# Second expert layer: where the halves of the next expert's weights are made, and three banks for the first products

## The chip, the core and the metric

The kernel runs on one core of a Trainium2 chip. The time is the device time of one execution in microseconds. Before the change it is 1087.37 us, the median of three runs (1087.16 to 1089.33). The core has five engines with a queue of instructions each, worked off in order: TensorE (PE in the rows; PEld is its weight load), VectorE (DVE), ScalarE (ACT), GpSimd (POOL) and SyncE (SP), which here issues the loads. Engines wait for each other by semaphores. TensorE writes its sums into PSUM, eight banks of 512 fp32 columns; ScalarE and VectorE read them there.

## The reference

Attention with normed queries and keys, then a first layer of eight experts with a free choice of expert for each token, then a second layer of eight experts in which each expert gets exactly 224 tokens. The change is in the second layer alone:

```python
def _moe2_ref(x, w_gate, w1, w2):          # x [1792, 768], w1 [8, 768, 1024], w2 [8, 1024, 768]
    cap = N // E                           # 224
    logits = x @ w_gate
    # pairs (token, expert) by falling logit; a token takes the first expert with room
    ...
    for e in range(E):
        mask = assigned == e
        h = np.maximum(x[mask] @ w1[e], 0.0)
        out[mask] = h @ w2[e]
```

All of it is fp32, and the result has to be near fp32 too.

## The kernel before

The second layer is `moe2`. It works the experts off one by one, in the order in which the assignment closes them (n = 0 to 7 below; "expert 6" is the seventh that is worked off). The assignment itself runs on all engines beside the experts, a few experts ahead (`pace`; lines up to L1908). An expert has 32 steps t.

*First products*, t = 0 to 15: h = relu(x W1), transposed. Eight products f, each of 128 rows of h by 224 tokens, summed over six pieces k of W1; two steps for a product. *Second products*, t = 16 to 31: h W2 in two halves of 112 tokens, each over eight pieces k of W2, in two column halves.

Experts 0 and 1 take fp32 operands as they are. From expert 2 on (`n >= NAT`) every operand is the sum of a high half, which TensorE takes at a higher rate, and the low rest. `split` (L2057 on) makes the two halves of one piece of a weight: ScalarE copies the piece into the high half (L2063, `w1h`, `w2h`), VectorE subtracts that from the piece into the low half (L2065, `w1l`, `w2l`). Then a first product is, per k, one wide matmul of the high half of W1 with both halves of x (448 columns, L2104) and a narrow one of the low half (224 columns, L2105); a second product is three matmuls (L2135 to L2137). What a first product leaves has to be summed and split as well (`relu2`): ScalarE copies one part (`hr`, L2110), VectorE adds the other (L2112), ScalarE makes the high half of relu (`hh`, L2114), VectorE the low half (`hl`, L2116). With the sum (L2112) the product's bank is free again.

The pieces of weights go through six buffers (`raws`, tiles `qkv`): 14 pieces an expert, six of W1 and then eight of W2, loaded in order by SP (`pump`, L2039), each as soon as the half six pieces earlier is made. W1's fourth piece is held back until the gather of the next expert's tokens has been issued on POOL, by a memset of one element there. There is one set of halves of W1 and one of W2, so those of the next expert can be written only when the present expert has read that piece for the last time.

`turn` (L2075) brings the gathered tokens of the next expert into x transposed, in four parts: three transposes into bank `px0`, then ScalarE's copy (`xx`, L2085) and VectorE's difference (L2088). All four use the one bank `px0`.

What sets the order around the change is the loop of `experts` (L2183 on). It runs at build time and issues each engine's instructions in the order that stands; it carries estimated clocks of the engines, with which `ahead(t)` decides whether a gather, a turn or a half is issued at a step. In the kernel before:

- `ahead` (L2187), from t = 17 on: a turn's transposes at one step, its copy and difference at the next; halves of W1 of the next expert at odd steps only, and not at a step on which transposes were issued, so in effect once the turns are done.
- After the 32 steps: the halves of W1 that are left, then the first two of W2 (L2259 to L2263).
- In the first products, at even t: `relu2` of the product before, and then half t/2 + 2 of W2 (L2210 to L2214).
- `product(f)` (L1989) gives product f the bank f mod 2 of `pg2`.

Of the kernel before, what the change touches and what calls it, by code (L numbers as in the profile page):

```python
# [22 lines left out]
N, DM, E, FF = 1792, 768, 8, 1024  # L23
# [1329 lines left out]
class Pace:  # L1353
# [49 lines left out]
    def work(self, eng, cost, ready=0.0):  # L1403

        clock = self.clock
        start = max(clock["p"], clock[eng], ready)
        self.until(start + SLACK if eng == "p" else min(start, clock["p"] + AHEAD))
        clock[eng] = max(start, clock[eng]) + cost
        return clock[eng] + SYNC
# [551 lines left out]
def moe2(tc, consts, qkv, x0, asn, w1, w2, y, out):  # L1961
# [10 lines left out]
    with ExitStack() as ctx:  # L1972
# [13 lines left out]
        zr = x0[0]  # L1986
        xgs = [p2.tile([CP, YW], F32, name=f"xg{i}") for i in range(2)]

        def product(f):  # L1989
            return pg2[f % 2][:, : 2 * CAP]  # L1990

        def first_product(f):

# [41 lines left out]
        def piece(i):  # L2035
            n, k = divmod(i, KD + KF)
            return n, k < KD, k if k < KD else k - KD
# [69 lines left out]
        def relu2(pg, f):  # L2107
            hr, hh = rows["hr"][f % NHR], rows["hh"]
            t = work("s", 0.36, max(done[f], there.get(("h", f - NHR), 0.0)))
            nc.scalar.activation(hr, pg[:, CAP:], AF.Copy)  # L2110
            t = work("v", 0.38, t)
            nc.vector.tensor_tensor(out=hr, in0=pg[:, :CAP], in1=hr, op=OP.add)  # L2112
            t = work("s", 0.33, t)
            nc.scalar.activation(hh[:, f, :], hr, AF.Relu)  # L2114
            there["h", f] = work("v", 0.36, t)
            nc.vector.scalar_tensor_tensor(hl[:, f, :], hr, 0.0, hh[:, f, :].bitcast(F32), op0=OP.max, op1=OP.subtract)  # L2116
# [37 lines left out]
        def experts(compact):  # L2154
# [26 lines left out]
                for _ in g:  # L2181
                    pass
            for n in range(E):  # L2183
                splits = iter(range(KD) if NAT <= n + 1 < E else ())
                turns, gathered, turned = [], 0, 0

                def ahead(t):  # L2187

                    nonlocal gathered, turned
                    if n + 1 == E:  # L2190
                        return
                    if known > n + 1 and gathered < 2:
                        gather(n + 1, gathered)
                        gathered += 1
                    elif t >= 17:
                        if turned < 4 and gathered > turned // 2 and ready[turned // 2] <= clock["p"]:
                            if len(turns) == turned:
                                turns.append(turn(n + 1, turned))
                                next(turns[turned])
                                return  # L2200
                            for _ in turns[turned]:
                                pass
                            turned += 1
                        if t % 2 and arrival and nload > nsplit + direct and arrival[piece(nsplit + direct)] <= clock["p"] + EARLY:
                            k = next(splits, None)
                            if k is not None:
                                split(n + 1, True, k)

                for t in range(32):
                    if n and t % 2 == 0 and 2 <= t <= 16:  # L2210
                        f = t // 2 - 1
                        relu(product(f)[:, :CAP], f) if n < NAT else relu2(product(f), f)
                    if n >= NAT and t % 2 == 0 and t // 2 + 2 < KF:
                        split(n, False, t // 2 + 2)  # L2214
                    if n and t == 3:
                        store(n - 1, 1)
                    if t == 25:
                        store(n, 0)
                    ahead(t)
                    pump()  # L2220
                    if t < 16:
                        if n:
                            f, a = divmod(t, 2)
                            for k in range(3 * a, 3 * a + 3):
                                acc(n, product(f)[:, :CAP], f, k) if n < NAT else acc2(n, product(f), f, k)
                        elif t < 6:

                            k, a = divmod(t, 2)
                            for f in range(4 * a, 4 * a + 4):
                                acc(n, first_product(f), f, k, True)  # L2230
                        elif t < 6 + KF:
                            f = t - 6
                            for k in range(3, KD):
                                acc(n, first_product(f), f, k, True)

                            for i in range(f - 1, f + 1) if f % 2 else ():
                                relu(first_product(i), i)
                    else:
                        gemm2(n, (t - 16) // 8, t % 8)
# [16 lines left out]
                        clock["p"] = max(clock["p"], ready[turned // 2])  # L2256
                    ahead(17)
                pump()
                for k in splits:  # L2259
                    split(n + 1, True, k)  # L2260
                if n + 1 >= NAT:
                    split(n + 1, False, 0)
                    split(n + 1, False, 1)  # L2263
            store(E - 1, 1)
            for r in room:
                r.close()
# [14 lines left out]
NAT = 2  # L2281
# [72 lines left out]
```

## Time and profile before

| | |
|---|---|
| median of 3 runs | 1087.37 us |
| the profiled execution | 1089.45 us |
| its span, first to last instruction | 1087.5 us |
| mean granted TensorE clock over the span | 0.958 |
| TensorE busy | 1016.0 us, 93% |
| VectorE busy | 601.5 us, 55% |
| ScalarE busy | 506.6 us, 47% |
| 16 DMA engines moved | 151.05 MB, mean 139 GB/s |

The span is read from the first to the last instruction of one execution; busy times are shares of it. The mean over the whole kernel says little of one stage: experts 2 to 7 of the second layer run from about 849 to 1075 us, and views with a window show that part alone. The granted clock is the share of TensorE's 2.4 GHz that the chip let through; 0.50 is its lower level of 1.2 GHz. In a row that shows idle time, the arrow names what ended it.

### The profile page before, as it was taken

What the parts mean: (1) busy time and instruction counts of PE and PEld (TensorE: products, weight loads), DVE (VectorE), ACT (ScalarE), POOL (GpSimd) and SP (SyncE); (2) the same over time, 40 slices, a digit from 0 to 9 for tenths busy, and PEclk for the clock granted to TensorE, in tenths of its full rate; (3) what the DMA queues carried; (4) which work ended last, traced back from release to release, by engine and by line L of the source; (5) the groups of instructions that cost most, each with busy time, mean ns of one, the idle gap of its engine ahead of it and who ended that gap; (6) DMA issues with size and microseconds to landing.
All of it is one profiled execution on the core that took longest, in us unless ns stands there. A gap on an engine that the chain in (4) does not pass through costs nothing. (4 is left out here: it accounts for less than half of the span.)

```text
span 1087.5 us, 19047 instructions
## 1 busy us (share of the span) xinstructions
PE 1016.0 (93%) x6224; PEld 785.1 (72%) x6224; DVE 601.5 (55%) x1664; ACT 506.6 (47%) x1127; POOL 238.3 (22%) x228
## 2 busy tenths in 40 slices
PE   7999999999999699999999998949999999999895
PEld 6555555555565588888888997738575789889885
DVE  5776877877875931111322121585778766565470
ACT  3777677777776322221352222641212555464460
POOL 5444333333323410001060111010111011021000
PEclk7899999999999899999999999867999999899998
DMA  6566556566556036436630011015930854775540
GB/s 154 123 145 146 130 140 146 129 145 147 124 154 200 5 92 246 157 137 238 222 117 32 31 59 36 16 52 219 323 101 18 266 181 150 237 228 157 182 143 28
DMA packets 80898, 151.05 MB, mean 139 GB/s; under 512 B 14254, under 2 KB 53422, under 8 KB 80752
## 3 DMA queue, kind: packets, MB, share of 16 engines
q1 hardware_dynamic: 75552, 126.06, 39.4%
q0 software_dynamic: 5200, 23.33, 6.7%
q8 instruction: 56, 0.92, 0.4%
q14 instruction: 90, 0.74, 0.2%
HBM read 110.69 MB, written 17.44 MB: 118 GB/s over the span
## 5 line engine op out<-in xcount | busy, mean ns | idle before, releaser
L205 DVE TENSOR_REDUCE nm<-sp 112x1 f32<-112x448 f32 x192 | 117.8, 618 | 56.9 <-PE sp L204 29.2
L211 ACT ACTIVATE e<-sp,nm 112x448 f32<-112x448 f32 x192 | 121.8, 634 | 54.1 <-DVE nm L205 34.9
L2104 PE MATMUL bank<-xx,w1h 128*128 128x448 f32 x288 | 101.9, 403 | 13.9 <-DVE hr L2112 13.8
L219 PE MATMUL tp<-ident,e 112*112 112x112 f32 x768 | 112.0, 269 | 0.6 <-DVE et L222 0.6
L219 PEld LDWEIGHTS tp<-ident,e 112*112 112x112 f32 x768 | 82.0, 135 | 26.4 <-issue 20.0
L232 PE MATMUL op<-et,qkv 112*64 112x448 f32 x384 | 99.3, 564 | 0.0
L225 ACT ACTIVATE et<-tp 112x448 f32<-112x448 f32 x144 | 78.4, 546 | 36.6 <-PE tp L219 35.1
L908 PE MATMUL po<-w2h,hh 128*128 128x384 f32 x240 | 85.9, 358 | 0.1
L200 PE MATMUL sp<-bt,at 128*112 128x448 f32 x188 | 85.6, 455 | 0.4 <-DMA bt<-cut 0.3
L880 PE MATMUL pg<-w1h,xh 128*128 128x512 f32 x180 | 75.8, 421 | 7.4 <-PEq L1192 6.0
L909 PE MATMUL po<-w2l,hh 128*128 128x384 f32 x240 | 81.8, 341 | 0.0
L911 PE MATMUL po<-w2h,hl 128*128 128x384 f32 x240 | 79.9, 338 | 0.0
L2105 PE MATMUL bank<-xx,w1l 128*128 128x224 f32 x288 | 79.1, 275 | 0.0
L2104 PEld LDWEIGHTS bank<-xx,w1h 128*128 128x128 f32 x288 | 57.2, 198 | 26.3 <-DVE hr L2112 21.2
L2143 POOL DMA_INDIRECT out_dram<-x,ids x16 | 17.2, 1074 | 254.3 <-ACT x L2142 129.3
L137 POOL TENSOR_TENSOR xn<-qkv,rr 112x512 f32<-112x512 f32 x47 | 48.0, 1053 | 112.7 <-DVE rr L128 112.7
L882 PE MATMUL pg<-w1h,xl 128*128 128x512 f32 x180 | 71.9, 399 | 0.0
L881 PE MATMUL pg<-w1l,xh 128*128 128x512 f32 x180 | 71.8, 399 | 0.0
L200 PEld LDWEIGHTS sp<-bt,at 128*112 128x112 f32 x188 | 33.9, 181 | 47.3 <-issue 32.0
L2135 PE MATMUL bank<-w2h,hh 128*112 128x384 f32 x192 | 66.3, 345 | 0.0
L896 DVE TENSOR_TENSOR hl<-ph,hh 128x512 fp32r<-128x512 f32 x30 | 20.7, 690 | 80.6 <-ACT hh L893 48.8
L2137 PE MATMUL bank<-w2h,hl 128*112 128x384 f32 x192 | 64.7, 337 | 0.0
(438 smaller groups left out, 2180.6 us busy)
## 6 DMA issues: line engine op xcount, KB each, us to landing
qkv<-in_moe_w_dram SPq DMA_DIRECT2D x88, 384.0 KB, 6.0
qkv<-in_moe_w_dram SPq DMA_DIRECT2D x36, 512.0 KB, 4.5
raw<-in_moe_w_dram SPq DMA_DIRECT2D x24, 512.0 KB, 6.6
bt<-cut SPq DMA_DIRECT2D x96, 112.0 KB, 2.3
at<-cut SPq DMA_DIRECT2D x96, 112.0 KB, 2.3
w1s<-in_moe_w_dram SPq DMA_DIRECT2D x12, 512.0 KB, 6.6
w2s<-in_moe_w_dram SPq DMA_DIRECT2D x16, 384.0 KB, 9.1
qkv<-in_v_dram SPq DMA_DIRECT2D x12, 448.0 KB, 6.7
```

Of the source, the lines that this page charges most:

```text
L200: nc.tensor.matmul(sp, lhsT=at[:, h, cs], rhs=bt[:, h, :], start=h == 0, stop=h == 1)
L205: nc.vector.tensor_reduce(out=st["nm"][:, n : n + 1], in_=sp, axis=AX.X, op=OP.max, negate=True)
L211: nc.scalar.activation(e, st.pop(("s", n)), AF.Exp, bias=st["nm"][:, n : n + 1], accum_out=st["sm"][:, n : n + 1])
L219: nc.tensor.transpose(tp[:, kc, :], e[:, kc * CP : (kc + 1) * CP], ident[:CP, :CP])
L225: nc.scalar.activation(dst, tp, AF.Copy)
L232: nc.tensor.matmul(st["op"][h * D : (h + 1) * D, :], lhsT=raws[i // 2][:, 2, 2 * (i % 2) + h, kc * D : (kc + 1) * D], rhs=st["et"][:, h, k ...
L880: nc.tensor.matmul(pg, lhsT=xh[:, k, :], rhs=w1h[:, k, fs], start=k == 0, stop=False)
L908: nc.tensor.matmul(po[n], lhsT=hh[:, k, :], rhs=w2h[:, kk, cs], start=kk == 0, stop=False)
L909: nc.tensor.matmul(po[n], lhsT=hh[:, k, :], rhs=w2l[:, kk, cs], start=False, stop=False)
L911: nc.tensor.matmul(po[n], lhsT=hl[:, k, :], rhs=w2h[:, kk, cs], start=False, stop=kk == KF - 1)
L2104: nc.tensor.matmul(pg, lhsT=h[:, k, fs], rhs=xx[:, k].rearrange("p a c -> p (a c)"), start=k == 0, stop=False)
L2105: nc.tensor.matmul(pg[:, :CAP], lhsT=l[:, k, fs], rhs=xh[:, k, :], start=False, stop=k == KD - 1)
```

## The change

Three things are changed, all for experts 2 to 7.

1. `ahead` issues halves at every step from 17 on, beside a turn too, in the order of the pieces: the six of W1, and from t = 26 on those of W2 as well, where the present expert's second products are past the piece (`what[2] <= t - 25`; for expert 2's own W2 not, since the memory is then still expert 1's). What is left of W1 and the first two of W2 follow after the 32 steps as before, and what is left of W2 goes beside the first products, one at each even step.
2. `relu2` pauses after the sum, and the half of W2 is issued there: between `hr` with its sum and `hh`, no longer behind `hl`.
3. The first products go round three banks, the two of `pg2` and `px0`, which the turns use in the second products.

```diff
-        def product(f):
-            return pg2[f % 2][:, : 2 * CAP]
+        def product(n, f):
+            if n < NAT:
+                return pg2[f % 2][:, :CAP]
+
+            return (pg2 + [px0])[f % 3][:, : 2 * CAP]
...
             nc.vector.tensor_tensor(out=hr, in0=pg[:, :CAP], in1=hr, op=OP.add)
+            yield
             t = work("s", 0.33, t)
             nc.scalar.activation(hh[:, f, :], hr, AF.Relu)
...
-                splits = iter(range(KD) if NAT <= n + 1 < E else ())
...
                                 turns.append(turn(n + 1, turned))
                                 next(turns[turned])
-                                return
-                            for _ in turns[turned]:
-                                pass
-                            turned += 1
-                        if t % 2 and arrival and nload > nsplit + direct and arrival[piece(nsplit + direct)] <= clock["p"] + EARLY:
-                            k = next(splits, None)
-                            if k is not None:
-                                split(n + 1, True, k)
+                            else:
+                                for _ in turns[turned]:
+                                    pass
+                                turned += 1
+                        what = piece(nsplit + direct)
+                        if what[0] == n + 1 and (what[1] or n >= NAT and t > 25 and what[2] <= t - 25) and nload > nsplit + direct and arrival[what] <= clock["p"] + EARLY:
+                            split(*what)
...
-                        relu(product(f)[:, :CAP], f) if n < NAT else relu2(product(f), f)
-                    if n >= NAT and t % 2 == 0 and t // 2 + 2 < KF:
-                        split(n, False, t // 2 + 2)
+                        sums = relu2(product(n, f), f) if n >= NAT else relu(product(n, f), f)
+                        if sums:
+                            next(sums)
+                    what = piece(nsplit + direct)
+                    if n >= NAT and t % 2 == 0 and what[:2] == (n, False):
+                        split(*what)
+                    if n >= NAT and t % 2 == 0 and 2 <= t <= 16:
+                        next(sums, None)
...
-                for k in splits:
-                    split(n + 1, True, k)
-                if n + 1 >= NAT:
-                    split(n + 1, False, 0)
-                    split(n + 1, False, 1)
+                while n + 1 >= NAT and (piece(nsplit + direct)[1] or piece(nsplit + direct)[2] < 2):
+                    split(*piece(nsplit + direct))
```

Line numbers rise by three from `first_product` on and by four behind `relu2`: the wide first product is L2104 before and L2107 after, the sum L2112 and L2115, the halves L2063 and L2065 before and L2066 and L2068 after.

How the order moves on VectorE beside expert 6's second products, before (`xx` a turn's difference, `w1l` and `w2l` low halves of expert 7's weights; `bank_11364` is `px0`):

```order
L2088 TENSOR_TENSOR xx<-bank_11364,xx 128x3x112 x4
L2065 TENSOR_TENSOR w1l<-qkv_88,w1h 128x1024 x2
L2065 TENSOR_TENSOR w1l<-qkv_87,w1h 128x1024 x3
L2065 TENSOR_TENSOR w1l<-qkv_88,w1h 128x1024
L2065 TENSOR_TENSOR w2l<-qkv_88,w2h 128x768 x2
```

And at the same place in the changed program, up to the first products of expert 7:

```order
L2068 TENSOR_TENSOR w1l<-qkv_88,w1h 128x1024
L2091 TENSOR_TENSOR xx<-bank_11364,xx 128x3x112
L2068 TENSOR_TENSOR w1l<-qkv_88,w1h 128x1024
L2068 TENSOR_TENSOR w1l<-qkv_87,w1h 128x1024
L2091 TENSOR_TENSOR xx<-bank_11364,xx 128x3x112
L2068 TENSOR_TENSOR w1l<-qkv_87,w1h 128x1024 x2
L2091 TENSOR_TENSOR xx<-bank_11364,xx 128x3x112
L2068 TENSOR_TENSOR w1l<-qkv_88,w1h 128x1024
L2091 TENSOR_TENSOR xx<-bank_11364,xx 128x3x112
L2068 TENSOR_TENSOR w2l<-qkv_88,w2h 128x768 x2
L2068 TENSOR_TENSOR w2l<-qkv_87,w2h 128x768 x3
L2068 TENSOR_TENSOR w2l<-qkv_88,w2h 128x768 x2
```

The four differences stood in a row ahead of all halves; now one or two halves of W1 stand ahead of each, and seven halves of W2 follow. TensorE's transposes stand where they stood, two steps apart.

ScalarE at the change from expert 6 to expert 7, before (`x` is the copy of a finished result for the store):

```order
L2063 ACTIVATE w2h<-qkv_88 128x768 x2
L2063 ACTIVATE w2h<-qkv_87 128x768
L2110 ACTIVATE hr_12573<-bank_11359 128x224
L2114 ACTIVATE hh<-hr_12573 128x224
L2063 ACTIVATE w2h<-qkv_87 128x768
L2142 ACTIVATE x_89<-bank_11363 112x384
L2142 ACTIVATE x_89<-bank_11361 112x384
L2110 ACTIVATE hr_12574<-bank_11360 128x224
L2114 ACTIVATE hh<-hr_12574 128x224
L2063 ACTIVATE w2h<-qkv_87 128x768
L2110 ACTIVATE hr_12575<-bank_11359 128x224
```

And changed:

```order
L2066 ACTIVATE w2h<-qkv_88 128x768 x2
L2066 ACTIVATE w2h<-qkv_87 128x768 x3
L2066 ACTIVATE w2h<-qkv_88 128x768 x2
L2113 ACTIVATE hr_12546<-bank_11359 128x224
L2066 ACTIVATE w2h<-qkv_88 128x768
L2118 ACTIVATE hh<-hr_12546 128x224
L2146 ACTIVATE x_89<-bank_11363 112x384
L2146 ACTIVATE x_89<-bank_11361 112x384
L2113 ACTIVATE hr_12547<-bank_11360 128x224
L2118 ACTIVATE hh<-hr_12547 128x224
L2113 ACTIVATE hr_12548<-bank_11364 128x224
L2118 ACTIVATE hh<-hr_12548 128x224
```

Before, three halves of W2 stand ahead of the first sum and one behind each of the five products that follow; changed, seven stand ahead and one follows, between `hr` and `hh`. The third product reads bank 11364, the turns' bank.

VectorE at the start of expert 3's first products in the changed program (`ns` is a small reduction of the assignment, which TensorE's matmul L1779 takes right behind product 0; before, it stood beside expert 1's second products):

```order
L2068 TENSOR_TENSOR w2l<-qkv_87,w2h 128x768
L2068 TENSOR_TENSOR w2l<-qkv_88,w2h 128x768 x3
L2068 TENSOR_TENSOR w2l<-qkv_87,w2h 128x768 x3
L1776 TENSOR_REDUCE ns<-u 128x8
L1782 SCALAR_TENSOR_TENSOR w<-w,u 128x64
L1784 TENSOR_REDUCE k<-w 128x8
L2115 TENSOR_TENSOR hr_12546<-bank_11359,hr_12546 128x224
L2068 TENSOR_TENSOR w2l<-qkv_88,w2h 128x768
```

Three small steps of the assignment have moved so, to behind the seventh half of W2: this one for expert 3, and two others for experts 4 and 5.

## Rows read from the trace of the kernel before

**Rows 1.** The page, costliest groups: busy, mean ns of one, idle before with releaser.

```profile
L2104 PE MATMUL bank<-xx,w1h 128*128 128x448 f32 x288 | 101.9, 403 | 13.9 <-DVE hr L2112 13.8
```

**Rows 2.** Stages by window: length, busy by engine, granted clock, DMA share, GB/s.

```profile
849.49:868.60 19.11, 17.02 (x98) 14.52 (x97) 14.10 (x24) 9.84 (x22) 1.04 (x2) 1.00 0.86 270
...
886.98:907.24 20.26, 17.74 (x97) 15.77 (x97) 13.80 (x24) 10.56 (x23) 1.04 (x2) 0.92 0.89 288
...
925.33:946.41 21.08, 18.59 (x98) 17.00 (x97) 13.26 (x23) 10.87 (x23) 1.04 (x2) 0.84 0.86 280
...
964.78:984.04 19.26, 16.74 (x97) 14.36 (x97) 12.42 (x22) 10.56 (x23) 1.04 (x2) 1.00 0.92 294
...
1002.00:1022.84 20.84, 17.74 (x97) 15.70 (x97) 12.72 (x23) 10.64 (x24) 1.04 (x2) 0.92 0.88 285
1022.84:1040.80 17.96, 17.96 (x111) 17.71 (x109) 9.57 (x12) 10.50 (x16) 0.97 (x1) 1.00 0.34 102
1040.80:1058.30 17.50, 16.31 (x97) 14.35 (x97) 12.48 (x23) 10.26 (x23) 0.94 (x1) 1.00 0.38 133
```

**Rows 3.** TensorE in order of time, first products: start, length, idle before.

```profile
892.86 0.47 PE L2104 MATMUL bank<-xx,w1h 128*128 128x448 f32 x1 [1.93 <-DVE hr L2112]
...
969.65 0.47 PE L2104 MATMUL bank<-xx,w1h 128*128 128x448 f32 x1 [0.92 <-DVE hr L2112]
...
1002.00 0.36 PE L2104 MATMUL bank<-xx,w1h 128*128 128x448 f32 x1
...
1005.68 0.27 PE L2105 MATMUL bank<-xx,w1l 128*128 128x224 f32 x1
1008.46 0.47 PE L2104 MATMUL bank<-xx,w1h 128*128 128x448 f32 x1 [2.51 <-DVE hr L2112]
```

**Rows 4.** ScalarE in order of time, first products of expert 6.

```profile
1006.27 0.84 ACT L2063 ACTIVATE w2h<-qkv 128x768 fp32r<-128x768 f32 x1 [1.91 <-DMA qkv<-in_moe_w_dram]
...
1012.05 0.34 ACT L2110 ACTIVATE hr<-bank 128x224 f32<-128x224 f32 x1
1013.47 0.39 ACT L2114 ACTIVATE hh<-hr 128x224 fp32r<-128x224 f32 x1 [1.08 <-DVE hr L2112]
```

**Rows 5.** VectorE in order of time, same stretch: one round of the loop.

```profile
1013.06 0.38 DVE L2112 TENSOR_TENSOR hr<-bank,hr 128x224 f32<-128x224 f32 x1
1013.90 0.39 DVE L2116 SCALAR_TENSOR_TENSOR hl<-hr,hh 128x224 fp32r<-128x224 f32 x1 [0.46 <-ACT hh L2114]
1014.63 0.96 DVE L2065 TENSOR_TENSOR w2l<-qkv,w2h 128x768 fp32r<-128x768 f32 x1 [0.34 <-ACT w2h L2063]
1015.51 0.38 DVE L2112 TENSOR_TENSOR hr<-bank,hr 128x224 f32<-128x224 f32 x1
```

**Rows 6.** A window of two microseconds in expert 4's first products, columns as rows 2.

```profile
934.00:936.00 2.00, 2.00 (x9) 1.87 (x8) 1.20 (x3) 1.48 (x3) 0.79 (x1) 0.50 0.74 168
```

**Rows 7.** TensorE in order of time, transposes beside expert 6's second products.

```profile
1023.89 0.45 PE L2081 MATMUL bank<-ident,xg 112*128 112x112 f32 x3
...
1026.27 0.45 PE L2081 MATMUL bank<-ident,xg 112*128 112x112 f32 x3
```

**Rows 8.** ScalarE in order of time, second products of expert 6.

```profile
1023.92 0.39 ACT L2114 ACTIVATE hh<-hr 128x224 fp32r<-128x224 f32 x1 [0.46 <-DVE hr L2112]
...
1032.96 5.79 ACT L2063 ACTIVATE w1h<-qkv 128x1024 fp32r<-128x1024 f32 x6
1039.08 0.85 ACT L2063 ACTIVATE w2h<-qkv 128x768 fp32r<-128x768 f32 x1 [0.33 <-DMA qkv<-in_moe_w_dram]
```

**Rows 9.** VectorE in order of time: expert 1's, then expert 6's second products.

```profile
827.84 0.50 DVE L2088 TENSOR_TENSOR xx<-bank,xx 128x336 fp32r<-128x336 f32 x1
828.26 1.20 DVE L1853 TENSOR_SCALAR g<-i,k 128x112 bf16<-128x112 bf16 x7
...
1034.04 6.90 DVE L2065 TENSOR_TENSOR w1l<-qkv,w1h 128x1024 fp32r<-128x1024 f32 x6 [1.53 <-ACT w1h L2063]
```

**Rows 10.** Loads into the six buffers, 1000 to 1048 us.

```profile
DMA to landing us min/median/max: 3.7/5.0/7.0
```

More of the change, by code (lines that the diff above doesn't have):

```diff
@@ L2224, in experts @@
                             for k in range(3 * a, 3 * a + 3):
-                                acc(n, product(f)[:, :CAP], f, k) if n < NAT else acc2(n, product(f), f, k)
+                                (acc if n < NAT else acc2)(n, product(n, f), f, k)
                         elif t < 6:
```

## The prediction

> **What bounds the kernel now.** I read the page's list of the costliest groups first: the idle time of TensorE in the stage that is changed is 13.9 us in front of the wide first products, 13.8 of it ended by VectorE's sum of the product halves (`hr`, L2112) [rows 1]. Then the time by stage, cut at the first matmul of each stage of experts 2 to 7 [rows 2]. The reader is to see two things there. In the second products TensorE is busy all the time (17.96 of 17.96 us), so nothing can be won there. In the first products it is not: the six stages last 19.11, 20.26, 21.08, 19.26, 20.84 and 17.50 us, 118.05 in all.
>
> What they would last without waits is read where TensorE runs freely, in the first two products of expert 6 [rows 3]: from the first wide matmul (1002.00) to the twelfth narrow one (1005.68) pass 3.68 us, and the next would be issued 0.10 later. So 12 pairs take 3.78 us, one pair 0.315, the 48 pairs of a stage 15.1; with 0.2 for the change of stage, 15.3. Six such stages are 91.8 us. The stages lose 118.05 - 91.8 = 26.25 us.
>
> Where it goes: product 2 of expert 6 waits 2.51 us for VectorE [rows 3]. Product f needs the bank of product f - 2, and that sum stands on ScalarE and VectorE behind halves of W2 whose weights have not landed (ScalarE waited 1.91 us for the DMA) [rows 4]. After that the two engines run a loop: from VectorE's sum at 1013.06 to the next at 1015.51 are 2.45 us [rows 5], because ScalarE's `hh` waits for the sum (1.08 us), the half of W2 stands behind `hh`, VectorE's half behind ScalarE's, and the next sum behind that [rows 4, 5]. TensorE needs only 6 x 0.315 = 1.89 us a product. The long waits have a second price. Two microseconds after such a wait the granted clock stood at 0.50, the 1.2 GHz level [rows 6]; the stages of experts 3, 4 and 6, where a wait was 1.93 to 2.51 us long, show 0.92, 0.84 and 0.92, the others 1.00 [rows 2, 3]. The largest waits of expert 5, 0.92 us, left it at 1.00 [rows 2, 3]. At (1 - clock) x length that is 1.6 + 3.4 + 1.7 = 6.7 us of the 26.25.
>
> **The change, part by part.** *Third bank.* Product f now needs the bank of f - 3, so its sum may end 1.9 us later than before. *Order in the products.* ScalarE's half of W2 stands between `hr` and `hh`, so it waits for no sum, and VectorE's row per product is sum, half, `hl`. That is 0.38 + 0.96 + 0.39 = 1.73 us, under 1.89, and ScalarE's 0.34 + 0.84 + 0.39 = 1.57 is too [rows 4, 5]: the loop is gone even for expert 2, which keeps five halves beside its products. *Earlier halves.* For experts 3 to 7 seven of the eight halves of W2 stand before the first sum and one behind it. All six stages should come down to 15.3 us: 26.25 us gained. I bound this: at most all of it; at least what the third bank alone would leave if the 2.45 us loop stayed, 8 x 2.45 = 19.6 a stage, which is nothing. I take all of it, since only one product per expert has a half beside it.
>
> *What hides the moved halves.* They now lie beside the second products, where VectorE was busy 9.57 of 17.96 us and ScalarE 10.50 [rows 2]. By the order of the changed program VectorE there makes 6 halves of W1, 4 turns, and then 6 to 7 halves of W2. W2's half k may be written only when TensorE has last read piece k, one step of about 1.05 us after another, and one half costs VectorE 0.96: it keeps up. The seventh piece of W2 is loaded into a buffer that the first half of W2 frees. With T the start of the second products, TensorE is done with piece 0 after 9.5 steps of 1.05 us, four turns of 2.38 - 2.10 = 0.28 and the 1.4 of waits worked out below [rows 7], at T + 12.5. ScalarE's half ends 0.85 later, VectorE's another 0.96, at 14.3. A load took 3.9 us (VectorE's first half of W1 ended at 1034.04 + 1.15 = 1035.19, ScalarE had the next piece at 1039.08) [rows 8, 9], so it lands at 18.2, and VectorE has made its half at 20.0, about 0.7 us into the next first products, which begin at 17.96 + 1.38 = 19.3. Their first sum is due 1.9 us in at the earliest. This costs nothing, but the cover is thin (rival C).
>
> *What the moved halves delay.* This is the price. The turns (three transposes into one bank, ScalarE's copy, VectorE's difference) used to come first on both engines, with the halves of W1 behind them; TensorE's transposes were 1026.27 - 1023.89 = 2.38 us apart and waited for nothing [rows 7]. Now two halves of W1 stand between two turns, and the next turn's transposes wait until VectorE has read the bank, with all second products queued behind them on TensorE. Six halves took VectorE 6.90 us, 1.15 each, and a difference 0.42 to the next start (827.84 to 828.26) [rows 9]. Two halves and a difference are 2.72 us against 2.38: each later turn waits 0.34. The first: `hh` of the last product starts at T + 1.08 (1023.92 - 1022.84) [rows 7, 8], the first half of W1 0.3 later at 1.4, VectorE's 1.08 behind it (1034.04 - 1032.96) [rows 8, 9] at 2.48, its difference at 3.63, done at 4.13 (0.50). The second transposes are due at 1.05 + 2.38 = 3.43 and wait 0.70. Together 0.70 + 0.34 + 0.34 = 1.38 us for each of experts 2 to 6, 6.9 us. Expert 1's second products (plain fp32, no halves) are longer, so its turns stand further apart and mostly find the bank free; of the 1.38 I put 0.4 there, an estimate between none and all of it. Bounds: nothing if VectorE runs ahead; if ScalarE's copy (0.39, as `hh`) never overlaps either, the two later waits are 2 x 1.15 + 0.50 + 0.39 - 2.38 = 0.81 each and the first 0.70 + 0.39 = 1.09, 2.71 an expert and 13.6 in all for five. I take 7.3, the value from back-to-back rows.
>
> *Waits that move.* Small matmuls of the assignment move from second into first products: no sum changes, but three of them now stand behind VectorE's seventh half (C). POOL's gathers keep their place ahead of the first products' stores, and the register loads on SP still come an expert early: nothing.
>
> Sum: 26.25 - 7.3 = 18.95 us. The profiled execution took 1089.45 us, so it would take 1070.5; the median of the runs is 2.08 us below it, so I predict 1087.37 - 18.95 = **1068.4 us**.
>
> A rule that speaks against the change: the Trainium skill, "TensorE: Matmul & The Clock Gate", section "HAM oscillation", reports that a second set of PSUM banks gave a kernel no further gain once its matmuls ran on. By it the third bank would be worth nothing here. The trace differs: it shows 13.8 us of waits for exactly that bank [rows 1].
>
> **The rivals.** *A, the forecast*: 1068.4, own range 1064 to 1073. *B, the turns don't wait*: VectorE ran in front of its order wherever rows let me see it; then 1087.37 - 26.25 = 1061.1. Against it: the 2.72 against 2.38 us come from back-to-back rows. *C, a late load*: loads took 3.7 to 7.0 us [rows 10]. At 7.0 the seventh piece lands at T + 21.3, 2.0 us into the first products; its two halves (0.85 + 0.96) and a small step of VectorE's, no longer than a sum (0.38), later an assignment matmul of experts 3, 4 and 5 that is due at 1.9 can run at 4.2. That is a wait of 2.3 us, long enough for the clock to fall, another 1.7 as in expert 6's stage [rows 2]. Three times 4.0 is 12: 1080.4. *D, no change*: C together with the turns' upper bound gives back 12 + 13.6 = 25.6 of 26.25: 1086.7. *E, slower by the clock*: if the waits of 0.3 to 0.7 us at the turns made the clock fall as expert 4's wait did, (1 - 0.84) x 21.08 = 3.4 us each time, twice beside each of five experts' second products, 34 us would be lost: 1102.4. It decides from six such stretches on. Against it stand expert 5's waits of up to 0.92 us at a clock of 1.00 [rows 2, 3].
>
> For E speaks the same page of the Trainium skill, section "A second HAM failure mode": frequent short idles between groups of matmuls, while banks are cycled, let the clock swing. By that the time would be E's; expert 5's stage contradicts it here.
>
> **How the numbers follow.** A 0.63, B 0.14, C 0.15, D 0.03, E 0.05. A run of this kernel is told from no change from about 0.2% (2.2 us) on. A, B and C are faster: 0.92; D is the same: 0.03; E slower: 0.05. The range reaches from B, 1061, to C, 1081.
>
> **What would show it.** Right: first-product stages of 15.2 to 15.6 us at clock 1.00, next to no wait of the wide first products for `hr`; second products of 19.0 to 19.7 us with waits of the transposes for `xx`, some 7 us in all, the first of a stage the longest; ScalarE's DMA waits beside the first products gone. Wrong: transposes that don't wait (B); assignment matmuls of experts 3 to 5 that wait 2 us for VectorE (C); a clock below 1.00 in second products (E); or the 2.45 us step between sums surviving beside most products, by which the gain itself would be missing.

## The result, and the profile after

The changed kernel took 1077.77 us, the median of eight runs (1072.99 to 1085.25), beside 1089.52 us for eight runs of the kernel before. The ratio is 0.9911, 95% interval 0.9894 to 0.9929: a gain of 9.7 us by the ratio, 11.75 by the medians, 11.03 between the two profiled executions (1089.45 and 1078.42). Forecast were 18.95. The direction was right, but four tenths of the gain (by the medians) to half of it (by the ratio) are missing: the time lies outside the forecast's own range of 1064 to 1073, between rivals A (1068.4) and C (1080.4) and nearer to C.

The wide first products, which were held up 13.8 us before [rows 1], now wait for nothing. From the page:

```profile
L2107 PE MATMUL bank<-xx,w1h 128*128 128x448 f32 x288 | 93.7, 381 | 0.0
```

The stages by window, columns as in [rows 2]. In order: expert 2's first and second products, the first products of experts 3 and 4, expert 5's first and second products, expert 6's first products.

```profile
850.39:865.89 15.50, 15.50 (x102) 14.68 (x99) 12.17 (x23) 9.46 (x23) 1.05 (x2) 1.00 0.79 270
865.89:885.24 19.35, 18.61 (x111) 17.48 (x109) 15.38 (x21) 14.08 (x20) 2.88 (x4) 1.00 0.67 199
885.24:901.75 16.51, 15.45 (x99) 14.46 (x98) 10.17 (x38) 7.58 (x18) 1.05 (x2) 1.00 0.65 242
...
921.21:941.97 20.76, 17.04 (x99) 15.89 (x99) 9.03 (x30) 7.47 (x18) 1.06 (x2) 0.92 0.55 190
...
961.31:977.76 16.45, 15.77 (x105) 14.86 (x104) 8.06 (x21) 7.58 (x18) 1.06 (x2) 1.00 0.63 236
977.76:997.10 19.34, 18.62 (x111) 17.46 (x109) 14.90 (x18) 14.08 (x20) 2.87 (x3) 1.00 0.67 199
997.10:1012.28 15.18, 15.18 (x97) 14.34 (x97) 7.13 (x16) 7.29 (x18) 1.06 (x2) 1.00 0.69 255
```

Two things are to be seen. Where TensorE runs freely (expert 6, 15.18 us; expert 7, 15.19) the first products take what the forecast said. Experts 3, 4 and 5 do not: 16.51, 20.76 and 16.45. And every second-product stage of experts 2 to 6 takes 19.34 to 19.46 us where it took 17.96 to 18.38, with TensorE idle for 0.45 to 0.75 us of each by its matmul rows.

| read from the stages | before | after | difference | forecast |
|---|---|---|---|---|
| first products, experts 2 to 7 | 118.05 | 99.59 | -18.46 | -26.25 |
| second products, experts 2 to 6 | 90.76 | 96.83 | +6.07 | +6.9 |
| second products, expert 1 | 25.53 | 26.22 | +0.69 | +0.4 |

The rest between the two spans, +0.6, lies ahead of and behind these stages. So the first products miss 7.8 us. The second products came out 0.8 us better than forecast: nine of the 16 small matmuls of the assignment that stood beside those of experts 2 to 6 are no longer there. TensorE's waits show where the 7.8 us went, in order of time (start, length, idle before):

```profile
866.94 0.45 PE L2084 MATMUL bank<-ident,xg 112*128 112x112 f32 x3
870.04 0.51 PE L2084 MATMUL bank<-ident,xg 112*128 112x112 f32 x3 [0.57 <-DVE xx L2091]
872.73 0.51 PE L2084 MATMUL bank<-ident,xg 112*128 112x112 f32 x3
...
888.35 0.17 PE L1779 MATMUL bank<-ns,ones 128*128 128x8 bf16 x1 [1.06 <-DVE ns L1776]
...
926.98 0.17 PE L1878 MATMUL bank<-fb,ut 128*128 128x8 bf16 x1 [3.72 <-DVE fb L1874]
...
964.31 0.22 PE L1858 MATMUL bank<-place,g 128*112 128x32 bf16 x1 [0.68 <-DVE g L1853]
```

The last three are the assignment matmuls of rival C, one in each of experts 3, 4 and 5. Expert 4's wait seen from ScalarE, VectorE and SyncE:

```profile
925.01 0.84 ACT L2066 ACTIVATE w2h<-qkv 128x768 fp32r<-128x768 f32 x1 [4.86 <-DMA qkv<-in_moe_w_dram]
```

```profile
925.88 0.96 DVE L2068 TENSOR_TENSOR w2l<-qkv,w2h 128x768 fp32r<-128x768 f32 x1 [4.74 <-ACT w2h L2066]
926.76 0.17 DVE L1874 TENSOR_SCALAR fb<-busyn 128x8 bf16<-128x8 f32 x1
```

```profile
916.43 0.33 SPq L2057 DMA_DIRECT2D qkv<-in_moe_w_dram  x1
```

The seventh piece of W2 was issued at 916.43, and ScalarE could take it at 925.01. VectorE waits for ScalarE's half; the small step `fb` of the assignment stands behind VectorE's; TensorE stands before `fb`. About a microsecond later the granted clock was down to 0.50, the 1.2 GHz level:

```profile
928.50:930.50 2.00, 2.00 (x9) 1.87 (x8) 0.04 (x1) 0.36 (x1) 0.97 (x1) 0.50 0.99 309
```

How long that piece takes is in the DMA view. First the landing times (the last number) when the window holds only this issue, for experts 4, 6 and 7 (experts 3 and 5: 5.7 each); then packets, megabytes and share of the 16 engines by queue in the two microseconds from the issue, expert 4's and expert 7's (q0 carries gathers and stores, q1 the loads):

```profile
qkv<-in_moe_w_dram SPq DMA_DIRECT2D x1, 384.0 KB, 8.5
...
qkv<-in_moe_w_dram SPq DMA_DIRECT2D x1, 384.0 KB, 6.1
...
qkv<-in_moe_w_dram SPq DMA_DIRECT2D x1, 384.0 KB, 3.3
...
q0 software_dynamic: 81, 0.33, 70.6%
q1 hardware_dynamic: 11, 0.03, 9.9%
...
q1 hardware_dynamic: 63, 0.19, 43.7%
q0 software_dynamic: 36, 0.11, 15.7%
```

Expert 7 is the last, so no tokens are gathered beside its load and no weights of a next expert follow it. It alone, with 3.3 us, is near the forecast's 3.9.

### The profile page after: what moved, and what is told of

The parts are those of the page before. It is cut to its first block, busy times and chain, and to the rows that moved or that the text cites. A ratio compares the mean times of both kernels' runs of the same rounds, so it can differ in the third digit from the quotient of the medians.

```text
span 1076.4 us, 19072 instructions
## 1 busy us (share of the span) xinstructions
PE 1009.3 (94%) x6224; PEld 780.4 (73%) x6224; DVE 600.0 (56%) x1664; ACT 511.4 (48%) x1127; POOL 233.9 (22%) x228
## 5 line engine op out<-in xcount | busy, mean ns | idle before, releaser
L2107 PE MATMUL bank<-xx,w1h 128*128 128x448 f32 x288 | 93.7, 381 | 0.0
L2140 PE MATMUL bank<-w2l,hh 128*112 128x384 f32 x192 | 64.7, 337 | 0.0
```

The lines of the kernel that those rows point to most:

```text
L2107: nc.tensor.matmul(pg, lhsT=h[:, k, fs], rhs=xx[:, k].rearrange("p a c -> p (a c)"), start=k == 0, stop=False)
```

## The experiments

Theory 1: what is missing is rival C (a late seventh piece, with an assignment step behind its half), and the turns' price is as forecast. The rivals to it are in the expectations. The sums of six first-product and five second-product stages (experts 2 to 6) are from each kernel's one profile, the ratios from its comparison with the kernel before. Where a load's landing decides, the stages differ from run to run (the profiles of experiments 5, 8, 9 and 12 are their slowest runs: 1080.12, 1084.27, 1067.83 and 1079.94), so verdicts go by the ratios.

| kernel | median us | ratio (95%) | first | second |
|---|---|---|---|---|
| before (medians of the five comparisons) | 1086.96 to 1089.52 | | 118.05 | 90.76 |
| changed | 1077.77 | 0.9911 (0.9894 to 0.9929) | 99.59 | 96.83 |
| 1 seventh half behind the sum | 1069.55 | 0.9828 (0.9810 to 0.9847) | 91.99 | 97.21 |
| 7 gather later | 1069.48 | 0.9842 (0.9827 to 0.9857) | 92.11 | 96.77 |
| 2 one half between turns | 1075.03 | 0.9888 (0.9869 to 0.9907) | 101.01 | 93.22 |
| 3 edits 1 and 2 | 1068.98 | 0.9819 (0.9799 to 0.9840) | 96.33 | 92.00 |
| 5 turns on two banks | 1077.36 | 0.9900 (0.9879 to 0.9922) | 108.99 | 90.28 |
| 6 edits 1 and 5 | 1062.30 | 0.9773 (0.9758 to 0.9788) | 92.01 | 90.36 |
| 4 third bank alone | 1077.37 | 0.9903 (0.9884 to 0.9922) | 101.07 | 94.21 |
| 13 order alone | 1076.75 | 0.9894 (0.9870 to 0.9918) | 104.46 | 91.35 |
| 9 bank and order | 1064.70 | 0.9791 (0.9778 to 0.9804) | 93.80 | 91.40 |
| 14 edits 9 and 5 | 1065.54 | 0.9803 (0.9788 to 0.9819) | 92.67 | 90.78 |
| 8 changed, two banks | 1077.58 | 0.9898 (0.9880 to 0.9915) | 104.73 | 96.82 |
| 10 edit 6, two banks | 1065.63 | 0.9799 (0.9786 to 0.9813) | 94.34 | 90.40 |
| 11 edit 6, old order | 1073.94 | 0.9883 (0.9866 to 0.9899) | 93.45 | 97.97 |
| 12 edit 6, both old | 1077.47 | 0.9897 (0.9882 to 0.9913) | 99.77 | 97.99 |

**1. The seventh half behind the first sum.**

```diff
-... t > 25 and what[2] <= t - 25)
+... t > 25 and what[2] <= min(t - 25, 5))
...
-if n >= NAT and t % 2 == 0 and what[:2] == (n, False):
+if n >= NAT and t % 2 == 0 and t and what[:2] == (n, False):
```

> The changed kernel, but the seventh half of W2 (and the eighth) is issued behind the first sum, beside the first products; the sixth stays ahead. Theory 1 (of the 18.95 us forecast some 7.8 are missing in the first products of experts 3, 4 and 5, where 1.06, 3.72 and about 1 us are waited by an assignment matmul for a small step of VectorE that stands behind the seventh half, whose piece lands 5.8 to 8.6 us after its issue; in expert 4 the clock falls after it): all six first-product stages 15.2 to 15.6 us at clock 1.00 (the changed kernel: 15.5, 16.5, 20.8, 16.5, 15.2, 15.2); second products unchanged at 19.3; time some 7 to 8 us under the changed kernel's 1077.8, near 1070, 0.982 of before. Rival (two halves beside the products bring the loop of sum, half, hh, hl back, or the late load holds hh and with it the second products): first products of 16 us and more in most experts; 1076 to 1080.

As theory 1 said, to half a microsecond. With the late half out of the way the whole change gains 18.1 us by the medians and 18.7 by the ratio, beside the 18.95 forecast. Expert 4's first products:

```profile
918.89:934.22 15.33, 15.33 (x99) 14.41 (x99) 9.16 (x35) 7.25 (x18) 1.06 (x2) 1.00 0.68 251
```

**7. The gather later.** The halves stand as in the changed kernel; only the gather moves away from the load.

```diff
-if known > n + 1 and gathered < 2:
+if known > n + 1 and gathered < 2 and (n < NAT or t > 4):
```

> The changed kernel, but the gather of the tokens after next is issued at steps 5 and 6 of an expert instead of 0 and 1, so on POOL behind the store at step 3. It is to tell why the seventh piece of W2 lands 5.7, 8.5, 5.7 and 6.1 us after its issue in experts 3 to 6 and 3.3 us in expert 7, which has no gather and no W1 loads behind it. Theory G (the gather, issued 0.1 us before the load, holds the 16 DMA engines: in the two microseconds after the issue its queue has 74 to 97% of them): the piece lands after 3.3 to 4 us, before the first products begin; the waits of 1.06, 3.72 and 0.68 us go; first products 15.2 to 15.6, second products 19.3: 1069 to 1071. Theory W (the W1 loads issued behind it share the engines): it still lands after 5.7 us and more, 1076 to 1079.

Theory G. Expert 4's seventh piece landed in 3.3 us, not 8.5, and the stage was free:

```profile
qkv<-in_moe_w_dram SPq DMA_DIRECT2D x1, 384.0 KB, 3.3
```

```profile
918.59:933.92 15.33, 15.33 (x100) 14.41 (x99) 9.14 (x30) 6.51 (x17) 2.94 (x4) 1.00 0.77 254
```

In experts 3, 5 and 6, too, ScalarE's seventh half starts within 4.0 us of the issue and no longer waits for the transfer (5.7 to 6.2 us in the changed kernel). In both kernels the store stands 2.67 us ahead of expert 4's load, and the next three loads follow it by 0.9, 1.7 and 2.6 us, so neither of these makes the difference: theory W falls. The expectation's 74 to 97% for the other queue is too high for the two microseconds that it names: they were 63 to 77% in experts 3 to 6.

So two edits that share nothing, one at the half and one at the gather, give back the same 8 us. The Trainium skill, "DMA: Bandwidth & Descriptors", section "Queues, rings and completion order", says that each DMA engine takes turns between the queues that have work, a packet at a time. The changed kernel's trace is near even shares from the third microsecond behind the issue of expert 4's piece (57, 40 and 38% for the loads, 41, 58 and 49% for the other queue), but not in the second, where the loads had 20 and the other 54; in experiment 7, with the gather gone, the loads had 82% in the second microsecond.

**2. One half between two turns.**

```diff
     turns.append(turn(n + 1, turned))
     next(turns[turned])
+    return
...
-while n + 1 >= NAT and (piece(...)[1] or piece(...)[2] < 2):
+while n + 1 >= NAT and (piece(...)[1] or piece(...)[2] < 6):
```

> The changed kernel, but no half is issued at a step on which a turn's transposes are issued, so one half of W1 stands between two turns, not two; the first six halves of W2 are issued before the first products at the latest. Theory 1 (the second products are 1.4 us longer because a turn's bank is read by VectorE behind two halves, 2.72 us against TensorE's 2.38): one half and a difference are 1.15 + 0.42 = 1.57, so no wait; second products 17.9 to 18.1 instead of 19.3, five times 1.35 = 6.7 us, and about 0.6 in expert 1. The assignment's small steps of experts 3 to 5 also fall elsewhere here, not behind the seventh half, so theory 1 expects the 7.8 us of the first products back as well although the piece lands as late as before: 1062 to 1064. Rival a (the transposes wait for something else, a bank or the gather): second products stay at 19.3. Rival b (the late load itself stops TensorE, not the small step behind its half): expert 4's first products stay above 19 us; about 1070.

Half right. The transposes came 2.4 to 2.5 us apart but for two (2.66 and 3.19) and waited 0.2 us in all for `xx`. The time missed the 1062 to 1064: the second products took 18.4 to 19.0, with more of the assignment's small matmuls in experts 2, 4 and 5 and a wait of 0.71 us for `hl` in expert 6, and experts 2 to 5 waited in the first products, now at product 3, which needs the bank of product 0, whose sum stands behind the late seventh half (rival b's mechanism, smaller):

```profile
892.56 0.47 PE L2107 MATMUL bank<-xx,w1h 128*128 128x448 f32 x1 [2.12 <-DVE hr L2115]
```

**3. Both edits.**

> Both edits: one half of W1 between two turns, and the seventh and eighth half of W2 behind the first and second sum. Theory 1: first products 15.2 to 15.5, second products 17.9 to 18.1, so 26 us less than before less about 1: 1062 to 1064, and a smaller spread from run to run than the changed kernel's 1073 to 1085, since nothing of TensorE's waits for a transfer any more. Rival (the waits come back at the second and third sum): 1068 to 1072.

The rival's 1068 to 1072: waits of 0.5 to 0.6 us for `hr` come back in three stages, and halves and assignment steps are dealt out anew.

**5. The turns on two banks.** No half moves.

```diff
-turns.append(turn(n + 1, turned))
+turns.append(turn(n + 1, turned, [px0, pg2[0]][turned % 2] if n else px0))
```

> The changed kernel, but the four turns of experts 2 to 7 go alternately into px0 and the first bank of pg2, which is free in the second products; no half is moved. Theory 1 (the transposes wait for the one bank, because two halves stand between VectorE's reads of it): with a second bank VectorE may be a whole turn late, so no wait of the transposes; second products 18.0 to 18.1 instead of 19.3, first products as in the changed kernel (99.6 us in all, expert 4 with its wait of 3.7 us): 1077.8 - 6.7 - 0.5 = 1070 to 1072. Rival (VectorE or ScalarE is simply too late with the new x, and the first products wait instead): second products shorter, first products longer by as much, 1076 to 1079.

The waits of the transposes are gone, the second products are at 17.96 to 18.39, and the time is the changed kernel's: the rival's time, but not its reason, since no first product waits for the new x. The waits are again the assignment's, in experts 3, 4 and 5; expert 3's stage follows:

```profile
889.07 0.17 PE L1779 MATMUL bank<-ns,ones 128*128 128x8 bf16 x1 [4.12 <-DVE ns L1776]
...
927.79 0.17 PE L1878 MATMUL bank<-fb,ut 128*128 128x8 bf16 x1 [2.77 <-DVE fb L1874]
...
966.18 0.28 PE L1858 MATMUL bank<-place,g 128*112 128x32 bf16 x1 [3.10 <-DVE g L1853]
```

```profile
882.90:904.58 21.68, 17.56 (x98) 16.37 (x98) 10.24 (x39) 7.47 (x18) 1.06 (x2) 0.84 0.55 192
```

The granted clocks are 0.84, 0.91 and 0.84. Counted from the start of the second products, TensorE begins the first products 1.1 to 1.4 us sooner here, but the seventh piece is asked for sooner by as much (13.2 to 13.6 us into the second products, 14.6 to 14.7 in the changed kernel), so that alone would change no wait. What differs is the time from the issue to ScalarE's half, here expert 3's:

```profile
878.12 0.33 SPq L2057 DMA_DIRECT2D qkv<-in_moe_w_dram  x1
```

```profile
887.00 0.84 ACT L2066 ACTIVATE w2h<-qkv 128x768 fp32r<-128x768 f32 x1 [5.06 <-DMA qkv<-in_moe_w_dram]
```

It is 8.88, 7.64 and 8.15 us in experts 3, 4 and 5, beside 5.82, 8.58 and 5.73 in the changed kernel, and the differences of 3.1, -0.9 and 2.4 are those of TensorE's waits. For expert 3 the piece is issued 2.55 us behind the load before it, not 3.94, and in the microsecond before the issue the loads' queue held 74% of the engines, not 11%. That this crowding makes the load longer is not shown by a run of its own.

**6. Edits 1 and 5.**

> The seventh and eighth half of W2 behind the first and second sum, as in the first experiment, and the turns on two banks. Theory 1: first products 15.2 to 15.5 and second products 18.0 to 18.1 in every expert, the forecast's 26.25 us less some 1: 1061 to 1064. Rival (TensorE is no longer waited for, but its assignment matmuls now fall into these stages, or the late x is waited for): 1066 to 1069.

Theory 1: 1062.30, by the ratio 24.7 us under the kernel before (0.0227 of 1088.02). One expert of it, first and second products:

```profile
914.49:929.82 15.33, 15.33 (x99) 14.41 (x99) 9.37 (x36) 7.14 (x18) 1.05 (x2) 1.00 0.71 264
929.82:947.78 17.96, 17.96 (x111) 17.71 (x109) 15.87 (x24) 13.85 (x20) 2.86 (x3) 1.00 0.66 199
```

TensorE is busy throughout, at a clock of 1.00. It is the fastest version here. The piece is as late as in experiment 5 (7.8 to 8.2 us from the issue to ScalarE's half in experts 3 to 6) and costs TensorE nothing, since the assignment's step and the first sum now stand ahead of the half.

**4. The third bank alone.** The kernel before, with the diff's `product`.

> The kernel before with nothing but the third bank for the first products (halves and relu2 in the old order). Forecast of the prediction: the loop of 2.45 us from sum to sum stays, eight products take 19.6 us, so nothing is gained: 1087 to 1091, first products 19 to 21 us. Rival (the third bank lets the loop run behind TensorE and only the last two or three products feel it): one product more of slack is 1.9 us a stage, some 11 us in all, and the falls of the clock go as well: 1072 to 1078.

The prediction's bound, nothing gained, fell. The loop is there, 2.46 us from sum to sum, but TensorE feels it only from product 4 on (expert 3's, the first products began at 886.82):

```profile
894.48 0.39 DVE L2115 TENSOR_TENSOR hr<-bank,hr 128x224 f32<-128x224 f32 x1
896.94 0.38 DVE L2115 TENSOR_TENSOR hr<-bank,hr 128x224 f32<-128x224 f32 x1
```

```profile
894.93 0.47 PE L2107 MATMUL bank<-xx,w1h 128*128 128x448 f32 x1 [0.36 <-DVE hr L2115]
```

The waits of 1.9 to 2.5 us at product 2 are gone, and the falls of the clock with them. Against that, the second products grow by 3.45 us in all, with the transposes waiting once in each, 0.45 to 0.48 us, for `xx`.

**13. The order alone**, two banks, halves where they were (the `yield` of the diff and its two `next`).

> The kernel before with nothing but the new order in relu2 (the half of W2 between the sum and hh): two banks, halves where they were. Theory 2 (the gain of the change is the order's and the bank's, and either one of them or the earlier halves takes away only a part): the loop of 2.45 us is gone, but product 2 still waits for the first sum behind the late pieces of W2, 1.9 to 2.5 us in experts 3, 4 and 6 with falls of the clock, 0.9 in expert 5: stages of 15.5 to 19, some 103 in all against 118.05: 1071 to 1076. Rival (with two banks the order changes nothing, since each sum is needed within one product): 1085 to 1090.

Theory 2 held, its time just above the 1071 to 1076. One wait a stage is left in experts 3 to 6, at product 2, for the first sum behind late pieces:

```profile
891.41 0.47 PE L2107 MATMUL bank<-xx,w1h 128*128 128x448 f32 x1 [2.49 <-DVE hr L2115]
```

**9. Bank and order**, the halves where they were.

> The kernel before with the third bank and the new order in relu2 (the half of W2 between the sum and hh), but with the halves where they were. It is to tell whether the earlier halves are needed at all. If the loop of 2.45 us is the whole trouble once the third bank takes up the late pieces of W2 (VectorE's row is then 1.73 us a product against TensorE's 1.89): first products 15.2 to 16.0, second products 18.0 to 18.4 as in the kernel before, 1063 to 1067. If the pieces of W2 land too late for that (ScalarE waited up to 1.91 us for one in the kernel before, 14.5 us in all, and now hr of the next product stands behind it): 16 to 18 us in a stage, 1070 to 1077, no better than the bank alone.

The first reading. VectorE's sums of expert 2, with five halves beside its products, follow each other in 1.47 to 1.91 us; the steps of 2.45 are gone:

```profile
857.30 0.39 DVE L2115 TENSOR_TENSOR hr<-bank,hr 128x224 f32<-128x224 f32 x1 [0.29 <-ACT hr L2113]
859.21 0.38 DVE L2115 TENSOR_TENSOR hr<-bank,hr 128x224 f32<-128x224 f32 x1
860.68 0.38 DVE L2115 TENSOR_TENSOR hr<-bank,hr 128x224 f32<-128x224 f32 x1
862.22 0.38 DVE L2115 TENSOR_TENSOR hr<-bank,hr 128x224 f32<-128x224 f32 x1
```

Bank and order gain 22.3 us by the medians without the earlier halves (1086.96 in the comparison's own runs of before). These, as the change places them, take about half of that away again: the change as a whole is some 13 us slower than without its first part.

**14. Edits 9 and 5.**

> Third bank and new order as in the ninth experiment (1064.7), halves where they were in the kernel before, and the turns on two banks. The transposes waited once there, 0.34 us, so theory 2 expects only that and the difference of the small steps: 1062 to 1065, as the sixth experiment with its earlier halves (1062.3). Then the earlier halves are worth nothing beside bank and order. Rival (they are): 1066 to 1068.

Just above the 1062 to 1065 expected. Against experiment 6 (the intervals of the ratios only touch) the earlier halves are worth 3 us by the medians and 1 us by the stages when nothing stands behind the late one: 15.82 and 15.80 us in two stages here, 15.19 and 15.33 there, and 18.49 against 18.08 in expert 2.

**8. The change without the third bank.**

```diff
-return (pg2 + [px0])[f % 3][:, : 2 * CAP]
+return pg2[f % 2][:, : 2 * CAP]
```

> The changed kernel with two banks for the first products instead of three: the earlier halves and the new order in relu2 alone. By the prediction's own reading (the loop of 2.45 us and the late pieces are what costs, the bank only adds slack) most of the gain is there without the bank: stages of 15.2 to 16.5 us but for expert 4, where product 2 waits for a sum behind the late seventh half: 1077 to 1082. Rival (the bank alone does it, as the experiment with the bank alone, 1077.4, suggests, and the halves give nothing): first products of 19 us, 1085 to 1091.

As expected of the prediction's own reading. The waits are at the same three assignment matmuls (1.29, 2.86 and 2.96 us), and expert 7 takes 15.19: in the changed kernel the third bank adds nothing that can be measured.

**10. Edit 6 on two banks.**

> The kernel of the sixth experiment (seventh and eighth half behind the sums, turns on two banks; 1062.3) with two banks for the first products. Theory 1 now (with nothing but two halves beside the products and each sum ahead of the half, a sum is done 1.1 us after its product, and the bank is free 0.8 us before it is needed): the same, 1061 to 1064, first products 15.2 to 15.6. Rival (sum 1 stands on ScalarE and VectorE behind the late seventh half, and product 3 needs its bank): 1 to 3 us in each of experts 3 to 6, with falls of the clock 1068 to 1075.

1.6 us above the expectation: product 3 waits 0.3 to 0.7 us in experts 3, 4 and 6. Here the bank is worth 2 to 3 us (0.9799 against 0.9773, intervals that just touch). The Trainium skill's remark that more PSUM banks gave a kernel nothing ("TensorE: Matmul & The Clock Gate", section "HAM oscillation") agrees with experiment 8, and not with 4, where the bank alone gave 10 us: here it depends on what else is late.

**11 and 12. Edit 6 with the old order in relu2, on three and on two banks.**

> The kernel of the sixth experiment with the halves behind hl again, as in the kernel before; three banks. With two halves beside the products the loop runs for two products only, which three banks cover: the same, 1061 to 1064. Rival (the order decides): first products 15.8 to 16.5, 1065 to 1069.

> The kernel of the sixth experiment without the third bank and without the new order in relu2. If the earlier halves and the two banks of the turns are all that is needed: 1061 to 1064. If bank or order are needed once a late half stands between two sums: product 3 waits 0.5 to 3 us in experts 3 to 6: 1066 to 1075.

Both times, 1073.94 and 1077.47, lie outside both readings, so nothing follows on the order from them. The estimated clocks of the loop shift with it, small matmuls of the assignment now stand as late as beside expert 6's second products, and in experts 5 and 6 the transposes wait for the gathered tokens themselves (experiment 11):

```profile
1016.63 0.51 PE L2084 MATMUL bank<-ident,xg 112*128 112x112 f32 x3 [1.27 <-DMA xg<-y,ids]
...
1022.60 0.51 PE L2084 MATMUL bank<-ident,xg 112*128 112x112 f32 x3 [1.72 <-DVE xx L2091]
1024.56 0.47 PE L2107 MATMUL bank<-xx,w1h 128*128 128x448 f32 x1 [1.46 <-DVE xx L2091]
```

Experiment 12 has the same waits, up to 3.13 us, and then a clock of 0.85 in expert 7's first products. Only experiment 11's first products can be compared: 93.45 us against 92.01, so with three banks and two late halves the order is worth about 1.4. What the earlier halves would do without the new order stays open.

## What the prediction had right, and the step that failed

*What a free stage takes*: right. 15.3 us forecast, 15.2 to 15.6 measured wherever nothing waits, and the 26.25 us are there to be had: experiment 6 has 92.01 us of first products, the forecast 91.8.

*The loop of 2.45 us and its end by the new order*: right (experiments 9 and 13). The waits for `hr` are gone in the changed kernel.

*The turns' price*: right. 0.70 + 0.34 + 0.34 forecast; the transposes' starts above are 3.10 and 2.69 apart, so 0.72 and 0.31 over the 2.38, and the stage is 19.34 - 17.96 = 1.38 longer. Experiment 5 shows the cause, the one bank. Expert 1's part was 0.69, not 0.4.

*The step that failed*: "A load took 3.9 us", and so "This costs nothing, but the cover is thin (rival C)". The piece was asked for when forecast (14.6 us into the second products, forecast 14.3), but the loads of experts 3 to 6 took 5.7, 8.5, 5.7 and 6.1 us. The 3.9 came from [rows 8, 9], between experts 6 and 7, the one change of expert with no gather beside the load. The kernel before already showed the other price. These are its first six pieces of W2 with two gathers beside them (change from expert 5 to 6, issued from 996.50 on) and with none (from 6 to 7, issued from 1035.30 on), the last number the median time to landing:

```profile
qkv<-in_moe_w_dram SPq DMA_DIRECT2D x6, 384.0 KB, 6.8
...
qkv<-in_moe_w_dram SPq DMA_DIRECT2D x6, 384.0 KB, 4.1
```

In the changed kernel the piece is asked for at the end of W2's first half, and the gathers stand on POOL right behind the store of half the results, which the same second products release: they went out 1.4 and 0.15 us ahead of the load, for experts 3 to 6 every time. Moving the gather brought 3.3 us and the whole loss back (experiment 7). Rival C named the place, the three matmuls and the fall of the clock; its price of 4.0 us a time, from the 7.0 of [rows 10], was too high for experts 3 and 5 (1.3 and 0.9 over their stages in experiment 1) and too low for expert 4 (5.4); the three add up to 7.6. With 0.15 it was given too little: its first half, a longer load, had a row ([rows 10], up to 7.0), and its second half, the step behind the half, stood in the order.

*The lower bound of the first products*, that the third bank alone would bring nothing: wrong. 8 x 2.45 let the loop bind from the first product to the last. In experiment 4 TensorE feels it only from product 4 on, and the gain is 10 us.

*What carried the gain*: not weighed apart in the prediction. Bank and order reach 1064.7 by themselves; the earlier halves, which the sum also leaned on, are the part that cost.

*Rivals B, D and E*: the transposes did wait, against B, and at the forecast's price, not at the 13.6 us of D. Against E, no second-product stage of the changed kernel fell below a clock of 1.00, with single waits of 0.28 to 0.57 us at the turns.

## What to carry to other kernels

Price a moved transfer by a row where the same neighbours run beside it, and look in the order for what will be issued in the same two microseconds. When a wait is found, ask what stands in order behind the waiting instruction on its engine and which engine stands before that: here a 0.17 us step behind a late half stopped TensorE for 3.7 us. And before a change of several parts is judged, run the parts alone and the whole without each part: one mend alone can show nothing (experiment 5) and be worth 6 to 7 us once another loss is out of the way (experiment 6 against 1).

## What the runs showed of the hardware

A load of 384 KB landed in 3.3 us with no gather beside it (expert 7, and expert 4 in experiment 7) and in 5.7 to 8.5 us with two gathers issued 1.4 and 0.15 us before it (experts 3 to 6), at the same size and on the same queue.

The length of a wait did not decide alone whether the clock fell: a stage with one wait of 2.49 us kept 1.00 and one with 1.84 us showed 0.91 (both experiment 13); 1.93 us gave 0.92 in the kernel before [rows 3], and every first-product stage with a wait of 2.7 us or more showed 0.84 to 0.92.

The part ahead of expert 1's first products, in which no instruction differs, ended between 740.5 and 744.2 us in these profiles. A difference of 2 to 3 us between two profiled spans can therefore come from that part alone; sums over the stages concerned were surer.
